# A planned attention and FFN kernel: slack between engines past the first units, and a lead of three

## The chip, the cores and the metric

The kernel runs on one core of a Trainium2 chip. The metric is the device time of one execution in microseconds. Five engines matter here: TensorE (PE) multiplies matrices, VectorE (DVE), ScalarE (ACT) and GpSimd (POOL) work on elements, and SyncE (SP) issues the DMA transfers. Each engine runs its own instructions in the order in which the program lists them, and waits on semaphores for what other engines make.

## The reference, cut to what matters

```python
def _attn_ref(q, k, v):                       # (4, 8, 768, 64)
    k_sum = k.reshape(B, H, nb, 32, D).max(axis=3)
    v_sum = v.reshape(B, H, nb, 32, D).mean(axis=3)
    scores_l = scale * q @ k.T                # kept where |i - j| < 16
    scores_s = scale * q @ k_sum.T + log(32)
    a = softmax(concat(scores_l masked, scores_s))
    return a @ concat(v, v_sum)

def _moe_ref(x, w_in, w_out):                 # x (3072, 512), d_ff 2048
    h = x @ w_in
    g = h * (1.0 / (1.0 + np.exp(-h)))
    return g @ w_out
```

The attention of 4 batches and 8 heads gives 3072 tokens of 512 numbers, and a feed-forward network (FFN) with a hidden width of 2048 follows.

## The kernel before, in words

Attention works in 24 stages s of 128 tokens, six to a batch. A stage has four score groups m (two heads each): PE makes the scores (L544 for batch 0, L546 and L547 for the others), DVE adds the mask and takes the maximum (L551), ACT takes the exponential (L554), DVE the reciprocal of the sum (L559, L560). The weights p are then written as float16 by DVE, ACT or POOL (one helper: L569 on DVE, L565 on ACT, L567 on POOL), and DVE makes their low parts (L593, four instructions a group). A transposing DMA (L596) turns p, PE multiplies with v (L625, 40 matmuls a stage), and ACT and DVE write the result as xh and xl (L643, L644; L638, L639 in the first two stages). The q, k and v of batches 1 to 3 come by DMA and are split into two parts by ACT, DVE and POOL (L444 to L450, L506, L507, L210, L215).

The FFN works in units: 12 chunks c of 256 tokens times 16 slices f of the hidden width, 192 units. The list `order` sets their sequence: chunk 0 and chunk 1 with the first eight slices, then with the other eight, then chunks 2 to 11 one after another. Unit i is done by `job_f`:

- F1 (L699): 12 matmuls of 256 columns into a PSUM bank of a ring of three (two for chunks 0 and 1);
- tanh on ACT (L709) into a tile t of a ring of three;
- t = (t + 1) * h on DVE (L710), the last reader of the bank;
- gh, the rounded part, on ACT (L711), and gl, the rest, on POOL or DVE (L215), each in a ring of four;
- F2 (L704): two halves of three matmuls of 512 columns, into two PSUM banks that collect the chunk; at its end ACT or DVE copies them out (L730, L731).

Nothing of this is issued where it stands in the code. Each step is entered with `plan.op`: which engines may do it and its cost on each, what it reads and writes, and a priority. `Plan.schedule` makes a list schedule from these costs, `sweep`, forward and backward in turns, and `issue` writes the instructions out by planned start. The time from the end of one operation to the start of the next that needs it is `lag`: on one engine `SELF`, else `LAT` and small additions. The planned times are used for the order and for the choice of the engine alone; on the chip the semaphores decide. PE also gets filler matmuls (L285, L708) where the plan sees a gap in the first part.

The tuning numbers (`TUNE`) and the costs of the operations are the same in both kernels. Line numbers of the text are those of the kernel before; in the changed kernel L699 is L704, L704 is L709, L710 is L715, and L569 is L574.

Of the kernel before, what the change touches and what calls it, by code (L numbers as in the profile page):

```python
# [44 lines left out]
LAST = (2.0 ** -29 * (1 - 2.0 ** -8), -0.5 + 7.5 * 2.0 ** -8)  # L45
QF = 8
AHEAD = 0
NPL = 2
NSUP = 2


class Plan:
# [19 lines left out]
    def __init__(self, tc, fill):  # L72
        self.tc, self.fill = tc, fill
        self.ops, self.writer, self.readers = [], {}, {}

    def op(self, engines, fn, r=(), w=(), prio=0.0, cols=0, port=("dve", "pool"), fill=None):
        i = len(self.ops)
        deps = set()
        for key in r:
            deps.add(self.writer[key])  # L80
            self.readers.setdefault(key, []).append(i)
        for key in w:
            if key in self.writer:
                deps.add(self.writer[key])
            deps.update(self.readers.pop(key, ()))
            self.writer[key] = i
        deps.discard(i)
        self.ops.append((engines, fn, sorted(deps), prio, cols, port, fill))

    def lag(self, a, b):  # L90
        return (self.SELF if a == b else self.LAT)[a] + (self.LEAD if b == "dma" else 110 if b == "pe" and a != "pe" else 0)

    def stream(self, seen, t, cost, cols):

# [14 lines left out]
    def sweep(self, prio, on, back):  # L109

        n = len(self.ops)
        before, after = [o[2] for o in self.ops], self.users
        if back:
            before, after = after, before
        left = [len(d) for d in before]
        end, chosen = [0.0] * n, [None] * n
        free = {} if back else {"dma": 1680.0}
        shared = 0.0
        ready, seen, fills, filled, early, order = {}, {}, 0, self.FIRST, True, []

        def arrive(i):
            ready[i] = {e: max([end[d] + (self.lag(e, chosen[d]) if back else self.lag(chosen[d], e)) for d in before[i]], default=0.0)
                        for e in ((on[i],) if on else self.ops[i][0])}

        for i in range(n):
# [76 lines left out]
def local_attn_ffn(ctx: ExitStack, tc: tile.TileContext, qkT, qF, qD, kF, kD, v, vR, w, out):  # L202
# [113 lines left out]
    def nudge(tag, *at):  # L316
        return NUDGE.get("_".join((tag,) + tuple(str(x) for x in at)), 0.0)
# [369 lines left out]
    def job_f(i, c, f):  # L687
# [13 lines left out]
        def ffn2(u):  # L701
            def go(e):
                for q, (g, part) in enumerate(((gh, 0), (gh, 1), (gl, 0))):
                    nc.tensor.matmul(out=bank[ob[u]], lhsT=g[:, u * P:u * P + P], rhs=wt[f, 1][:, part, :], start=(opens and q == 0), stop=(closes and q == 2))  # L704
            return go

        plan.op({"pe": 1430}, ffn1, r=[(x, z, half) for x in ("xh", "xl") for half in range(2)] + [("w", f, 0), ("wl", f, 0)], w=[("bank", k)], prio=i + nudge("f1", i), cols=3072,
                fill=lambda: nc.tensor.matmul(out=h, lhsT=unit[:, :P], rhs=unit, start=True, stop=True))  # L708
        plan.op({"act": 264}, lambda e: nc.scalar.activation(out=t, in_=h, func=AF.Tanh, scale=0.5), r=[("bank", k)], w=[("t", j)], prio=i - TUNE["post"])  # L709
        plan.op({"dve": 335}, lambda e: nc.vector.scalar_tensor_tensor(out=t, in0=t, scalar=1.0, in1=h, op0=ALU.add, op1=ALU.mult), r=[("bank", k)], w=[("t", j)], prio=i - TUNE["post"], port=())  # L710
        plan.op({"act": 307}, lambda e: nc.scalar.copy(out=gh, in_=t), r=[("t", j)], w=[("gh", n)], prio=i - TUNE["post"])  # L711
        plan.op({"pool": 742, "dve": 340}, lambda e: less(e, gl, t, gh.bitcast(F32)), r=[("t", j), ("gh", n)], w=[("gl", n)], prio=i - TUNE["post"])
        for u in range(2):
            plan.op({"pe": 690}, ffn2(u), r=[("gh", n), ("gl", n), ("w", f, 1), ("wl", f, 1)], w=[("bank", ob[u])], prio=late, cols=1536)
        if closes and f == NFT - 1:  # L715
            stg, key = staging()
        for u in range(2 if closes else 0):
# [61 lines left out]
    for f in range(NFT):  # L779
        for kind in range(2):  # L780
            job_w(f, kind, need_f[f] - TUNE["w_dec"] + kind)
    for i, (c, f) in enumerate(order):
        d = min([d for d in range(c + 1, NCHUNK) if slot[d] == slot[c]], default=None)
        if d and f == (QF if c < NSUP else AHEAD):
            job_stage(2 * d)
            job_attn(2 * d, True)
            job_stage(2 * d + 1)
        job_f(i, c, f)
        if c == 0 and f == NFT - 1:
            spare[0] = 1  # L790
        if d and f == NFT - 1:
            job_out(2 * d, True)
            job_attn(2 * d + 1, True)
            job_out(2 * d + 1, True)
# [73 lines left out]
```

## Time and profile before

| | |
|---|---|
| median of 3 runs | 691.08 us (690.7 to 693.31) |
| the profiled execution | 690.36 us |
| its span, first to last instruction | 688.6 us |
| PE busy | 662.1 us, 96% |
| DVE, ACT, POOL busy | 488.3, 427.3, 213.5 us |
| data moved by DMA | 97.43 MB, mean 141 GB/s |

The span is the stretch that the trace covers; the time of the execution is a little longer. Busy is the time in which at least one instruction of an engine runs. Matmuls are pipelined, so one takes longer from start to end than it holds up the next one; the busy time of PE is therefore read with the weight loads (PEld) and the waits beside it.

### The profile page before, as it was taken

How to read it: one execution, taken by the hardware profiler on the slowest of the kernel's cores; microseconds unless marked ns; L12 is line 12 of the kernel's file. 1: busy time of each engine (PE TensorE's matmuls, PEld its weight loads, DVE VectorE, ACT ScalarE, POOL GpSimd, SP SyncE). 2: the span in 40 equal slices, each digit the busy share in tenths (PEclk: the TensorE clock that was granted, in tenths of full speed). 3: DMA queues.
4: the chain of work that ended last, by engine and by line, in shares of the span. 5: the costliest groups of instructions: out<-in, count | busy, mean ns of one | idle time of the engine just before them, and what ended most of it. 6: DMA issues, size and time to landing. Idle time of an engine off the chain costs nothing. (4 is left out here: it accounts for less than half of the span.)

```text
span 688.6 us, 14268 instructions
## 1 busy us (share of the span) xinstructions
PE 662.1 (96%) x4971; PEld 572.1 (83%) x4971; DVE 488.3 (71%) x1500; ACT 427.3 (62%) x1136; POOL 213.5 (31%) x265
## 2 busy tenths in 40 slices
PE   8989999998999999999899999989999999999997
PEld 3668888887987988988788988977888888999996
DVE  5897978599988458887987556999996694323222
ACT  5988997686867547656756545676673584332222
POOL 3143465233645234234342242434333222000000
PEclk9999999999999999999999999999999999999999
DMA  8889863957666643754566532764573252000000
GB/s 275 257 243 302 320 221 104 251 161 215 132 152 149 210 116 97 171 135 111 157 158 156 179 102 79 182 160 113 123 187 75 73 126 61 12 31 1 30 1 32
DMA packets 101355, 97.43 MB, mean 141 GB/s; under 512 B 76950, under 2 KB 80022, under 8 KB 101282
## 3 DMA queue, kind: packets, MB, share of 16 engines
q1 hardware_dynamic: 101282, 96.51, 51.3%
q8 instruction: 39, 0.64, 0.4%
q14 instruction: 34, 0.28, 0.1%
HBM read 70.34 MB, written 6.29 MB: 111 GB/s over the span
## 5 line engine op out<-in xcount | busy, mean ns | idle before, releaser
L699 PE MATMUL bank<-xh,wt 128*128 128x256 f32 x1536 | 302.3, 287 | 8.1 <-DVE t L710 7.3
L699 PEld LDWEIGHTS bank<-xh,wt 128*128 128x128 f32 x1536 | 248.9, 192 | 18.0 <-DVE t L710 11.8
L704 PE MATMUL bank<-wt,gh 128*128 128x512 f32 x768 | 244.5, 400 | 1.9 <-DVE raw L731 1.9
L699 PE MATMUL bank<-xl,wt 128*128 128x256 f32 x768 | 218.3, 284 | 0.4 <-DVE xl L644 0.4
L215 POOL TENSOR_TENSOR gl<-t,gh 128x256 fp32r<-128x256 f32 x117 | 104.8, 900 | 254.6 <-ACT gh L711 206.0
L704 PEld LDWEIGHTS bank<-wt,gh 128*128 128x128 f32 x768 | 134.9, 189 | 24.3 <-DVE raw L731 2.1
L699 PEld LDWEIGHTS bank<-xl,wt 128*128 128x128 f32 x768 | 147.7, 192 | 3.8 <-DVE xl L644 0.8
L704 PE MATMUL bank<-wt,gl 128*128 128x512 f32 x384 | 150.0, 391 | 0.0
L711 ACT CAST gh<-t 128x256 fp32r<-128x256 f32 x192 | 75.8, 399 | 73.6 <-PE bank L704 67.5
L710 DVE SCALAR_TENSOR_TENSOR t<-t,bank 128x256 f32<-128x256 f32 x192 | 79.1, 417 | 54.9 <-ACT t L709 53.8
L709 ACT ACTIVATE t<-bank 128x256 f32<-128x256 f32 x192 | 71.3, 377 | 57.6 <-DVE gl L215 29.4
L593 DVE SCALAR_TENSOR_TENSOR p<-e,sum,p 128x128 f16<-128x128 f32 x352 | 104.8, 359 | 2.4 <-ACT p L565 1.7
L554 ACT ACTIVATE e<-e,mx 128x182 f32<-128x182 f32 x192 | 84.1, 439 | 24.5 <-DVE mx L551 24.2
L704 PEld LDWEIGHTS bank<-wt,gl 128*128 128x128 f32 x384 | 72.1, 188 | 16.2 <-POOL gl L215 0.2
L215 DVE TENSOR_TENSOR gl<-t,gh 128x256 fp32r<-128x256 f32 x75 | 45.1, 601 | 50.1 <-ACT gh L711 48.1
L567 POOL TENSOR_SCALAR p<-e,sum 128x182 f16<-128x182 f32 x68 | 33.8, 502 | 91.4 <-DVE sum L560 33.0
L551 DVE CUSTOM_DVE_ANT_0 e<-bank,masks,qsc 128x182 f32<-128x182 f32 x144 | 52.8, 400 | 8.3 <-PE bank L547 7.8
L565 ACT ACTIVATE p<-e,sum 128x182 f16<-128x182 f32 x79 | 32.6, 441 | 17.0 <-DVE sum L560 9.3
L215 POOL TENSOR_TENSOR vv<-raw,vv 128x1024 f16<-128x1024 f32 x16 | 34.6, 2168 | 14.7 <-DVE vv L212 11.1
L554 ACT ACTIVATION_READ_ACCUMULATOR e<-e,mx 128x1 f32 x192 | 36.1, 188 | 0.0
L450 DVE SCALAR_TENSOR_TENSOR qk<-raw,qsc,qk 64x1264 f16<-64x1264 f32 x18 | 28.1, 1561 | 6.5 <-ACT qk L449 6.0
L546 PE MATMUL bank<-qk 128*128 128x182 f16 x144 | 29.1, 247 | 2.6 <-DVE mx L551 2.0
(125 smaller groups left out, 687.4 us busy)
## 6 DMA issues: line engine op xcount, KB each, us to landing
wt<-in_w_dram SPq DMA_DIRECT2D x32, 512.0 KB
raw<-in_kD_dram SPq DMA_DIRECT2D x18, 632.0 KB
raw<-in_v_dram SPq DMA_DIRECT2D x20, 512.0 KB
raw<-in_qD_dram SPq DMA_DIRECT2D x18, 512.0 KB
out_dram<-raw SPq DMA_DIRECT2D x24, 256.0 KB
raw<-in_kF_dram SPq DMA_DIRECT2D x12, 384.0 KB
raw<-in_qF_dram SPq DMA_DIRECT2D x9, 512.0 KB
raw<-in_vR_dram SPq DMA_DIRECT2D x12, 384.0 KB
```

Source lines behind the costliest of these rows:

```text
L215: eng[e].tensor_tensor(out=out, in0=in0, in1=in1, op=ALU.subtract)
L546: nc.tensor.matmul(out=sc[:, i, :NKEY], lhsT=qh[:, h, :], rhs=kst[:, h, :], start=True, stop=False)
L551: plan.op({"dve": 258 if b == 0 else 323}, lambda e, i=i: nc.vector.tensor_tensor_reduce(out=et[:, i, :], in0=sc[:, i, :NKEY], in1=mask, s ...
L554: plan.op({"act": 431}, lambda e, i=i, h=h: nc.scalar.activation(out=et[:, i, :], in_=et[:, i, :], func=AF.Exp, scale=-1.0, bias=mx[:, i:i ...
L565: nc.scalar.activation(out=out, in_=et[:, i, :], func=AF.Copy, scale=by)
L567: nc.gpsimd.tensor_scalar(out=out, in0=et[:, i, :], scalar1=by, scalar2=0.0, op0=ALU.mult, op1=ALU.add)
L593: nc.vector.scalar_tensor_tensor(out=pt[:, i, to:to + z - a], in0=et[:, i, a:z], scalar=su[:, i:i + 1], in1=pt[:, i, a:z], op0=ALU.mult, o ...
L699: nc.tensor.matmul(out=h, lhsT=wt[f, 0][:, part, ct * P:(ct + 1) * P], rhs=x[:, ct, :], start=(ct == 0 and q == 0), stop=(ct == NCT - 1 an ...
L704: nc.tensor.matmul(out=bank[ob[u]], lhsT=g[:, u * P:u * P + P], rhs=wt[f, 1][:, part, :], start=(opens and q == 0), stop=(closes and q == 2))
L709: plan.op({"act": 264}, lambda e: nc.scalar.activation(out=t, in_=h, func=AF.Tanh, scale=0.5), r=[("bank", k)], w=[("t", j)], prio=i - TUN ...
L710: plan.op({"dve": 335}, lambda e: nc.vector.scalar_tensor_tensor(out=t, in0=t, scalar=1.0, in1=h, op0=ALU.add, op1=ALU.mult), r=[("bank", ...
L711: plan.op({"act": 307}, lambda e: nc.scalar.copy(out=gh, in_=t), r=[("t", j)], w=[("gh", n)], prio=i - TUNE["post"])
```

## The change

Three things are added, all in the plan. Operations that belong to attention or to the loading of data carry, from unit 32 on (`SETTLED`), a slack: where an operand comes from another engine, `lag` adds 2500 ns when the reader runs on PE, and 800 ns when it runs on DVE, ACT or POOL. No slack is added between operations of one engine, or for a reader on the DMA queue. The operations of `job_f` get 800 ns on PE alone (`GATE_SLACK`). And a key `turn` makes F1 of unit i depend on the second half of F2 of unit i - 3 (`APART`), in all units from 3 on. Both are on PE, so this costs no instruction and no semaphore.

```diff
--- before.py
+++ after.py
@@ -45,7 +45,11 @@
 LAST = (2.0 ** -29 * (1 - 2.0 ** -8), -0.5 + 7.5 * 2.0 ** -8)
 QF = 8
 AHEAD = 0
+SETTLED = 32
+SLACK = {"pe": 2500, "dve": 800, "act": 800, "pool": 800}
+GATE_SLACK = 800
 NPL = 2
+APART = 3
 NSUP = 2
 
 
@@ -72,6 +76,7 @@
     def __init__(self, tc, fill):
         self.tc, self.fill = tc, fill
         self.ops, self.writer, self.readers = [], {}, {}
+        self.slack = {}
 
     def op(self, engines, fn, r=(), w=(), prio=0.0, cols=0, port=("dve", "pool"), fill=None):
         i = len(self.ops)
@@ -85,10 +90,10 @@
             deps.update(self.readers.pop(key, ()))
             self.writer[key] = i
         deps.discard(i)
-        self.ops.append((engines, fn, sorted(deps), prio, cols, port, fill))
-
-    def lag(self, a, b):
-        return (self.SELF if a == b else self.LAT)[a] + (self.LEAD if b == "dma" else 110 if b == "pe" and a != "pe" else 0)
+        self.ops.append((engines, fn, sorted(deps), prio, cols, port, fill, dict(self.slack)))
+
+    def lag(self, a, b, user):
+        return (self.SELF if a == b else self.LAT)[a] + (self.LEAD if b == "dma" else 110 if b == "pe" and a != "pe" else 0) + (0 if a == b else self.ops[user][7].get(b, 0))
 
     def stream(self, seen, t, cost, cols):
 
@@ -119,7 +124,7 @@
         ready, seen, fills, filled, early, order = {}, {}, 0, self.FIRST, True, []
 
         def arrive(i):
-            ready[i] = {e: max([end[d] + (self.lag(e, chosen[d]) if back else self.lag(chosen[d], e)) for d in before[i]], default=0.0)
+            ready[i] = {e: max([end[d] + (self.lag(e, chosen[d], d) if back else self.lag(chosen[d], e, i)) for d in before[i]], default=0.0)
                         for e in ((on[i],) if on else self.ops[i][0])}
 
         for i in range(n):
@@ -704,14 +709,14 @@
                     nc.tensor.matmul(out=bank[ob[u]], lhsT=g[:, u * P:u * P + P], rhs=wt[f, 1][:, part, :], start=(opens and q == 0), stop=(closes and q == 2))
             return go
 
-        plan.op({"pe": 1430}, ffn1, r=[(x, z, half) for x in ("xh", "xl") for half in range(2)] + [("w", f, 0), ("wl", f, 0)], w=[("bank", k)], prio=i + nudge("f1", i), cols=3072,
+        plan.op({"pe": 1430}, ffn1, r=[(x, z, half) for x in ("xh", "xl") for half in range(2)] + [("w", f, 0), ("wl", f, 0)] + ([("turn", i - APART)] if i >= APART else []), w=[("bank", k)], prio=i + nudge("f1", i), cols=3072,
                 fill=lambda: nc.tensor.matmul(out=h, lhsT=unit[:, :P], rhs=unit, start=True, stop=True))
         plan.op({"act": 264}, lambda e: nc.scalar.activation(out=t, in_=h, func=AF.Tanh, scale=0.5), r=[("bank", k)], w=[("t", j)], prio=i - TUNE["post"])
         plan.op({"dve": 335}, lambda e: nc.vector.scalar_tensor_tensor(out=t, in0=t, scalar=1.0, in1=h, op0=ALU.add, op1=ALU.mult), r=[("bank", k)], w=[("t", j)], prio=i - TUNE["post"], port=())
         plan.op({"act": 307}, lambda e: nc.scalar.copy(out=gh, in_=t), r=[("t", j)], w=[("gh", n)], prio=i - TUNE["post"])
         plan.op({"pool": 742, "dve": 340}, lambda e: less(e, gl, t, gh.bitcast(F32)), r=[("t", j), ("gh", n)], w=[("gl", n)], prio=i - TUNE["post"])
         for u in range(2):
-            plan.op({"pe": 690}, ffn2(u), r=[("gh", n), ("gl", n), ("w", f, 1), ("wl", f, 1)], w=[("bank", ob[u])], prio=late, cols=1536)
+            plan.op({"pe": 690}, ffn2(u), r=[("gh", n), ("gl", n), ("w", f, 1), ("wl", f, 1)], w=[("bank", ob[u])] + ([("turn", i)] if u else []), prio=late, cols=1536)
         if closes and f == NFT - 1:
             stg, key = staging()
         for u in range(2 if closes else 0):
@@ -780,12 +785,15 @@
         for kind in range(2):
             job_w(f, kind, need_f[f] - TUNE["w_dec"] + kind)
     for i, (c, f) in enumerate(order):
+        plan.slack = SLACK if i >= SETTLED else {}
         d = min([d for d in range(c + 1, NCHUNK) if slot[d] == slot[c]], default=None)
         if d and f == (QF if c < NSUP else AHEAD):
             job_stage(2 * d)
             job_attn(2 * d, True)
             job_stage(2 * d + 1)
+        plan.slack = {"pe": GATE_SLACK} if i >= SETTLED else {}
         job_f(i, c, f)
+        plan.slack = SLACK if i >= SETTLED else {}
         if c == 0 and f == NFT - 1:
             spare[0] = 1
         if d and f == NFT - 1:
```

How it moves instructions is seen at three places. The first is PE in the last chunks, past all score groups: the first matmul of each F1 (L699 before, L704 in the changed kernel; its bank is the output) and the first of each F2 (L704 before, L709 in the changed kernel; gh3 is the tile of unit 171, gh0 that of unit 172). Units 172 to 175 before:

```order
L699 MATMUL bank2_201<-xh1_185,wt_1297 128x256
...
L699 MATMUL bank0_199<-xh1_185,wt_1341 128x256
...
L699 MATMUL bank1_200<-xh1_185,wt_1401 128x256
...
L704 MATMUL bank4_203<-wt_943,gh1_192 128x512 x2
...
L704 MATMUL bank4_203<-wt_966,gh2_193 128x512 x2
...
L704 MATMUL bank4_203<-wt_1048,gh3_194 128x512 x2
...
L699 MATMUL bank2_201<-xh1_185,wt_1468 128x256
```

and units 172 to 175 in the changed kernel:

```order
L704 MATMUL bank2_201<-xh1_185,wt_1220 128x256
...
L709 MATMUL bank4_203<-wt_1145,gh2_193 128x512 x2
...
L704 MATMUL bank0_199<-xh1_185,wt_1298 128x256
...
L709 MATMUL bank4_203<-wt_1183,gh3_194 128x512 x2
...
L704 MATMUL bank1_200<-xh1_185,wt_1331 128x256
...
L709 MATMUL bank4_203<-wt_1267,gh0_191 128x512 x2
...
L704 MATMUL bank2_201<-xh1_185,wt_1418 128x256
```

Before, three F1 stand together and then the six halves of three F2; the F2 that stand between F1 of 174 and of 175 are those of units 169, 170 and 171 (gh1, gh2, gh3), and that of 172 comes after F1 of unit 177. In the changed kernel F1 and F2 take turns, and between F1 of units 172 and 173 stands F2 of unit 170.

The second place is PE before the first F1: fillers (L285 and L708; L290 and L713 in the changed kernel), scores (L544; L549), products with v (L610; L615), and F1 of unit 0. Before:

```order
L285 MATMUL bank0_199<-ident_96 128x256
L544 MATMUL bank6_205<-qk0_149 128x182 x2
L708 LDWEIGHTS ident_96
L708 MATMUL bank0_199<-ident_96 128x256
...
L708 MATMUL bank0_199<-ident_96 128x256
L699 MATMUL bank0_199<-xh0_184,wt_446 128x256
```

and in the changed kernel:

```order
L290 MATMUL bank0_199<-ident_96 128x256
L549 MATMUL bank6_205<-qk1_150 128x182 x2
L615 MATMUL bank7_206<-wt_92,wt_91 64x128 x8
...
L549 MATMUL bank6_205<-qk1_150 128x182 x2
...
L549 MATMUL bank6_205<-qk1_150 128x182 x2
L713 LDWEIGHTS ident_96
L713 MATMUL bank0_199<-ident_96 128x256
...
L713 MATMUL bank0_199<-ident_96 128x256
L704 MATMUL bank0_199<-xh0_184,wt_386 128x256
```

Before, a score group on qk0, which is the first of stage 4, stands directly ahead of F1 of unit 0, with three fillers between; in the changed kernel that group comes after F1 of unit 1, and four fillers are left.

The third place is DVE in the attention of batch 2, around the group with e0 and sum0: the reciprocal (L560; L565 in the changed kernel), p (L569; L574), its low parts (L593; L598), t (L710; L715). Before:

```order
L710 SCALAR_TENSOR_TENSOR t0_188<-t0_188,bank1_200 128x256
L559 TENSOR_SCALAR sum2_168<-sum2_168 128x2
L593 SCALAR_TENSOR_TENSOR p_175<-e0_172,sum0_166,p_175 128x128
...
L593 SCALAR_TENSOR_TENSOR p_175<-e0_172,sum0_166,p_175 128x54
L710 SCALAR_TENSOR_TENSOR t1_189<-t1_189,bank2_201 128x256
L560 RECIPROCAL sum2_168<-sum2_168 128x2
L569 TENSOR_SCALAR p_175<-e2_174,sum2_168 128x182
L593 SCALAR_TENSOR_TENSOR p_175<-e2_174,sum2_168,p_175 128x128
```

and in the changed kernel:

```order
L565 RECIPROCAL sum0_166<-sum0_166 128x2
L565 RECIPROCAL sum1_167<-sum1_167 128x2
L574 TENSOR_SCALAR p_175<-e0_172,sum0_166 128x182 x2
L574 TENSOR_SCALAR p_175<-e1_173,sum1_167 128x182
L598 SCALAR_TENSOR_TENSOR p_175<-e0_172,sum0_166,p_175 128x128
...
L598 SCALAR_TENSOR_TENSOR p_175<-e0_172,sum0_166,p_175 128x54
L715 SCALAR_TENSOR_TENSOR t1_189<-t1_189,bank2_201 128x256
```

Before, p of this group is made by another engine and DVE makes p of the next one alone; in the changed kernel DVE makes both weights of this group itself, and one of the next. Over the whole program p stands on DVE 88 times in the changed kernel and 29 before, on ACT 46 and 79, on POOL 42 and 68 (times of L569, L565 and L567 into p); all other counts move by a few, and the fillers go from 103 and 4 to 73 and 8.

## Rows read from the trace of the kernel before

**Rows 1.** The page: span, and busy time of four engines (share, instructions).

```profile
span 688.6 us, 14268 instructions
...
PE 662.1 (96%) x4971; PEld 572.1 (83%) x4971; DVE 488.3 (71%) x1500; ACT 427.3 (62%) x1136; POOL 213.5 (31%) x265
```

**Rows 2.** The chain that ended last: start us, us, what.

```profile
539.37 0.08 PE bank L547
...
605.83 1.24 PE bank L625 x40
...
644.42 2.87 PE bank L699 x24
647.29 2.07 PE bank L704 x9
```

**Rows 3.** Waits of PE from 161.9 us: who, for whom, us, times, longest.

```profile
PE bank L699 <- DVE t L710: 6.2, 10, 1.6
...
PE bank L546 <- DVE mx L551: 1.6, 1, 1.6
```

**Rows 4.** Waits of the weight loads (PEld) from 161.9 us.

```profile
PEld bank L699 <- DVE t L710: 10.2, 13, 2.1
...
PEld bank L704 <- DVE raw L731: 2.1, 1, 2.1
PEld bank L412 <- DVE vm L404: 1.6, 1, 1.6
PEld bank L383 <- DVE am L379: 1.1, 2, 0.6
```

**Rows 5.** Waits of all engines over the whole span, the longest that concern the FFN.

```profile
ACT gh L711 <- PE bank L704: 67.5, 38, 4.5
...
ACT t L709 <- DVE gl L215: 29.4, 46, 2.2
```

**Rows 6.** Timeline, 242 to 250 us: start, us, instruction [idle before <-releaser].

```profile
243.08 2.12 DVE L215 TENSOR_TENSOR gl<-t,gh 128x256 fp32r<-128x256 f32 x1 [0.28 <-issue]
...
245.22 0.38 ACT L709 ACTIVATE t<-bank 128x256 f32<-128x256 f32 x1 [2.24 <-DVE gl L215]
...
247.53 0.39 ACT L709 ACTIVATE t<-bank 128x256 f32<-128x256 f32 x1 [1.62 <-DVE gl L215]
...
249.19 0.41 DVE L710 SCALAR_TENSOR_TENSOR t<-t,bank 128x256 f32<-128x256 f32 x1
...
249.66 0.38 PE L699 MATMUL bank<-xh,wt 128*128 128x256 f32 x1 [0.25 <-DVE t L710]
```

**Rows 7.** Timeline at the first F1: PE, and the xl that it reads.

```profile
48.59 0.68 DVE L639 TENSOR_TENSOR xl<-bank,xh 128x512 fp32r<-128x512 f32 x1
...
49.98 0.85 PE L544 MATMUL bank<-qk 64*128 64x182 f32 x4 [2.08 <-DMA qk<-in_qkT_dram]
...
51.24 0.56 PE L699 MATMUL bank<-xh,wt 128*128 128x256 f32 x1
```

**Rows 8.** Two windows: length, busy by engine, PEclk, DMA share, GB/s.

```profile
50.80:54.20 3.40, 3.40 (x18) 3.27 (x18) 3.22 (x10) 2.73 (x4) 0.79 (x1) 0.50 0.68 219
340.90:344.30 3.40, 3.40 (x19) 3.30 (x18) 3.37 (x10) 3.08 (x13) 1.84 (x3) 0.50 0.43 117
```

**Rows 9.** Groups by line: count | busy us, mean ns | idle before.

```profile
L593 DVE SCALAR_TENSOR_TENSOR p<-e,sum,p 128x128 f16<-128x128 f32 x352 | 104.8, 359 | 2.4 <-ACT p L565 1.7 <-POOL p L567 0.5
...
L711 ACT CAST gh<-t 128x256 fp32r<-128x256 f32 x192 | 75.8, 399 | 73.6 <-PE bank L704 67.5 <-DVE t L710 4.4
...
L569 DVE TENSOR_SCALAR p<-e,sum 128x182 f16<-128x182 f32 x29 | 11.8, 406 | 2.5 <-DMA tt<-p 1.6 <-DVE sum L560 0.3
```

**Rows 10.** One line's instructions: min/median/max ns, first to last start.

```profile
L593 DVE SCALAR_TENSOR_TENSOR p<-e,sum,p x352: 256/336/2253, 28.8 to 599.7; 128x128 f16<-128x128 f32 x176
...
L215 POOL TENSOR_TENSOR gl<-t,gh x117: 722/741/1965, 57.1 to 651.8; 128x256 fp32r<-128x256 f32 x117
...
L215 POOL TENSOR_TENSOR vv<-raw,vv x16: 2139/2148/2341, 90.2 to 516.4; 128x1024 f16<-128x1024 f32 x16
```

## The prediction

> **What bounds the kernel now.** I read the page first. PE is busy for 662.1 of 688.6 us, DVE for 488.3, ACT for 427.3, POOL for 213.5 [rows 1]. So PE sets the time, and an order can only win what PE loses in waits. The chain that ended last says the same from its end: from 605 us on it is PE alone, F1, F2 and a last product with v back to back, where 24 F1 matmuls take 2.87 us and nine F2 matmuls 2.07 us [rows 2]. A unit is thus 1.44 us of F1 and two halves of 0.69 us, 2.82 us in all; 40 products with v take 1.24 us, and one of the four score matmuls of a group 0.08 us.
>
> Then the waits, by PE's matmuls and by its weight loads. From 161.9 us, where unit 32 starts, the matmuls wait 6.2 us for "DVE t" ahead of F1, ten times, and the weight loads 10.2 us, thirteen times [rows 3, 4]. The two are the same waits seen twice: a matmul's end is modelled late, so the first is a lower bound, and the loads, which stand directly ahead of the matmul, give the better size. DVE's t is the last reader of the bank that the next F1 fills, so this is a wait for a free bank. Next come a copy of the output banks (2.1 us), the sum of v (1.6), the scale of v (1.1) [rows 4], and scores for the maximum (1.6) [rows 3].
>
> Why is t late, when a ring of three banks should give 7.0 us (three units less one F1)? The list of all waits shows it: ACT's cast to gh waits 67.5 us for F2, in 38 places, and ACT's tanh 29.4 us for gl on DVE [rows 5]. PE's order lets F1 run up to ten units ahead of F2 (the ring of four gh, three t and three banks all full), so gh waits until F2 four units back has freed a tile, and all that stands behind gh on ACT waits with it. The timeline shows one such run: a gl that takes 2.12 us instead of its usual 0.42 holds the tanh that needs its tile for 2.24 us, the next tanh waits 1.62, t starts at 249.19 and F1 at 249.66 [rows 6]. Where the F1 come in a burst, as they do (the order has up to seven in a row), the bank of the first must come free within 2.9 us.
>
> **The change part by part.** *The lead of three.* F1 of unit i now stands behind the second half of F2 of unit i - 3. When that F2 runs, its gl, gh and t are long done, so the bank and the t tile of unit i - 3 are free and gh of unit i - 4 too: F1 cannot wait for "DVE t" any more, and neither gh nor tanh for the rings. It costs no instruction. The gain is the bank wait, 6.2 us by the one row and 10.2 by the other [rows 3, 4]; I take 9, nearer the row of the loads.
>
> What it exposes: F2 now waits for its own gl. Before, 20 us of PE work stood between F1 and F2 of a unit. In the new order I count 5.6 us in the last chunks (F2, F1, F2, F1) and 4.5 to 7 elsewhere. The chain in that gap is tanh 0.38, t 0.41 [rows 6], gh 0.40 [rows 9] and gl 0.74 on POOL [rows 10]: 1.9 us, some 2.3 with the hand-overs. So a delay of 3.3 us on ACT, DVE and POOL together is covered by the two units between; what is later stops PE. What is in front of t on DVE then counts. I added, from the new order, every DVE instruction between two t by the mean of its group, less 0.06 us each, because neighbours overlap by that (L593: mean 359 ns, but 104.8 / 352 = 298) [rows 9]. Over the old order this gives 486 us, where the page has 488.3. In the new order it gives 499. Against PE's work in the same stretches: units 24 to 40 DVE 56.6, PE 51.9; 64 to 96 DVE 96.0, PE 104.1; 112 to 152 DVE 128.4, PE 131.0; the rest is well below. So the first of them is short of DVE by 4.7 us, of which the cover takes some 3, and the third runs at 98%, where single lumps (xl, the splits of q and k, a late DMA ahead of them on ACT) will stop PE at times. I put down 2 for the first, 1 for the second and 2 for the third: 5 us of new waits, with bounds of 0 and 25 (below).
>
> *The slack of 2500 ns on PE.* Scores, products and the small scale matmuls of attention now stand later behind what they read. In the waits of the loads that is 1.6 for the sum of v and 1.1 for the scale [rows 4], together 2.7. I take 2.5; the lower bound is 0, should the tight places only move. The 1.6 us for the maximum [rows 3] fall in a stage that is still planned without slack and whose groups stand just as close; I leave them.
>
> *The output copy.* 2.1 us [rows 4], and soon after it comes one of two stretches of 3.4 us in which PE is granted half its clock, 1.2 GHz instead of 2.4 [rows 8]; that costs 1.7 us of work. At each end of a chunk an F1 now stands between the last F2 and the first of the next, 1.44 us in which the copy can run. I take 3.5 of the 3.8 together (0 if the copy is late all the same).
>
> *The slack of 800 ns on DVE, ACT and POOL.* It is charged only where an operand changes engine. The reciprocal is on DVE, so p on DVE is charged nothing and on ACT or POOL 800 ns: that is why DVE makes 59 more of them. At 0.41 us each [rows 9] less the overlap this is 20 us on DVE, partly given back by other moves; it is in the 499 above. It is hidden as long as DVE has gaps, and is the larger part of the new-wait bound where it has none.
>
> On p the trace and a rule differ in what they say. L593 takes 336 ns at the median and up to 2253, and POOL's subtraction for v takes 2148 [rows 10]. The Trainium skill (SBUF — State Buffer, Who interferes with whom) says that a DVE instruction with two SBUF inputs and a GpSimd instruction that reads SBUF exclude each other for a whole instruction. By it, 26 p fewer on POOL would spare DVE some blocking, while two more subtractions for v on POOL add up to 2.1 us each. The two nearly cancel and leave the sum as it is.
>
> *The start.* Until F1 of unit 0 neither slack applies, but the lead changes the planned priorities. Before, a score group of stage 4 waits 2.08 us for its DMA directly ahead of F1, which starts at 51.24, though xl was done at 48.59 + 0.68 = 49.27 [rows 7]. Now that group stands behind F1 of unit 1, and DVE's work up to that xl is the same within 0.3 us. F1 should start near 49.3. A half-clock stretch begins at 50.8 [rows 8], after the wait; it may go or move. I take 2.5 us (0 to 1.9 + 1.7 = 3.6).
>
> **The sum.** -9 - 2.5 - 3.5 - 2.5 + 5 = -12.5. The span goes from 688.6 to 676.1 us, and with the 1.8 us that lay around it the execution to 677.9. The median of three runs was 0.7 above the profiled one; I say 678.
>
> **The rivals.** *All gains, no new waits:* 10.2 + 2.7 + 3.8 + 3.6 = 20 off, 671 by the median. For it speaks that DVE's sum uses means, which hold some very long instructions; by L593's median, 336 ns [rows 10], the dense stretches are looser.
>
> *The waits only move:* F1 no longer waits for a bank, and F2 waits as long for gl, since what makes t late is not the order but ACT and DVE in front of it (the timeline's gl of 2.12 us is such a case). It then stands within 0.5% of before, about what a measurement here can tell from no change: 688 to 694, say 690. The Trainium skill (Perfetto Trace Analysis, Identifying Performance Opportunities) reads a repeated gap on the engine that should be full as too few buffers; by that the ring of three banks is the limit, and an order that keeps the ring earns nothing. Against it: 67.5 us of ACT's waits are for F2 itself [rows 5], which the order alone decides. Halfway to this case, with half of the gain gone, it is 684 to 687.5.
>
> *DVE becomes the bound, slower:* if DVE's neighbours do not overlap where it is dense, its sum by full means is 68 us in units 24 to 40, 116 in 64 to 96 and 128 in 120 to 152, against PE's 52, 104 and 106: 16 + 12 + 22 = 50 us in place of 5. With a lead of three PE follows DVE at once, and the time is 678 + 45 = 723; with half of the 50, which is the bound of 25 above, 698. It decides from the point at which DVE is 95% busy over 40 us on end; now it is at 71% over the whole [rows 1], and L593 with a mean of 359 ns and 298 of busy time each speaks against it [rows 9].
>
> **How the numbers follow.** The forecast, 672 to 684, has 0.55. All gains (671 or so, below 672) 0.13, half gone (684 to 687.5, still faster) 0.09, the waits move 0.13, slower 0.10. Faster by over 0.5%: 0.55 + 0.13 + 0.09 = 0.77; within: 0.13; slower: 0.10. For the range I leave out about one in ten on each side: 668 to 690; the forecast's own is 672 to 684.
>
> **What would show it.** The wait of F1 for "DVE t" at or near zero past unit 3, and ACT's gh for F2 likewise; these follow from the order, and their failing would mean that I misread it. In their place a wait of F2's loads for gl (POOL or DVE L220), 5 us in all, most of it in units 24 to 40 and 112 to 152. DVE busy near 500 us. F1 of unit 0 near 49.3 us. No half-clock stretch in mid kernel. The forecast is wrong if the F2 wait for gl goes past 15 us, or if DVE is at 95% over a stretch of 40 us; and the step most likely to fail is the size of the new waits, since three lumps in a row on DVE or a late DMA on ACT are in no sum of mine.

## The result, and the profile after

The changed kernel takes 681.9 us (median of four runs), the kernel before 691.4 us in four runs on the same chip: a ratio of 0.985, with a 95% interval of 0.983 to 0.988. So 1.5% of the time went, 9.5 us. The profiled execution took 681.8 us, with a span of 679.9 against 688.6. Of the kernels further down, slack_only ran twice in a slower state (700.32 and 701.69 us, granted clock 0.96 instead of 0.99), and these two runs are left out of its median.

The page of the changed kernel, span and busy times:

```profile
span 679.9 us, 14188 instructions
PE 660.3 (97%) x4945; PEld 571.1 (84%) x4945; DVE 500.8 (74%) x1550; ACT 417.2 (61%) x1103; POOL 215.4 (32%) x248
```

Beside [rows 1] PE does the same work, less 26 fillers, in a shorter span, and DVE is busy 12.5 us longer. The lines of the code moved by five: F1 is now L704, F2 L709, tanh L714, t L715, gh L716, gl L220, the scores L549, L551 and L552.

Waits of the changed kernel's matmuls from 125 us on, and below them those of its weight loads (engine, line, releaser, then us in total, times, longest):

```profile
PE bank L551 <- DVE mx L556: 5.1, 5, 1.6
PE bank L713 <- DVE t L715: 1.7, 1, 1.7
PE bank L709 <- POOL gl L220: 1.2, 2, 1.0
PE bank L709 <- DVE gl L220: 0.6, 1, 0.6
PE bank L709 <- ACT gh L716: 0.5, 2, 0.3
```

```profile
PEld bank L709 <- POOL gl L220: 4.0, 8, 1.4
...
PEld bank L709 <- ACT gh L716: 1.5, 3, 0.7
PEld bank L709 <- DVE gl L220: 1.3, 2, 1.0
```

The waits of F1 for t, 6.2 and 10.2 us in [rows 3, 4], are gone, and so are the output copy, the sum of v and the scale of v. Only a filler (L713) still waits for t once. New are F2's waits for gl and gh, and the scores of L551 wait 5.1 us for the maximum, all in units 31 to 40 but for one short one.

The waits of all engines in the changed kernel:

```profile
DVE t L715 <- ACT t L714: 100.9, 89, 2.6
ACT t L714 <- PE bank L704: 96.0, 85, 2.1
ACT gh L716 <- DVE t L715: 94.4, 125, 3.2
```

ACT's gh, which waited 67.5 us for F2 [rows 5], waits for t now: the chain of a unit is followed at once, step by step, as an order with a short lead makes it.

The start, on PE's timeline (start us, us, instruction, idle before it and releaser), and two windows of the half clock (length, then busy us of PE, PEld, DVE, ACT and POOL, granted clock, DMA share, GB/s):

```profile
47.45 1.04 PE L713 MATMUL bank<-ident 128*128 128x256 bf16 x4
48.14 0.56 PE L704 MATMUL bank<-xh,wt 128*128 128x256 f32 x1
50.39 0.58 PE L704 MATMUL bank<-xl,wt 128*128 128x256 f32 x1 [1.69 <-DVE xl L644]
```

```profile
44.40:54.60 10.20, 8.45 (x38) 6.67 (x37) 8.94 (x26) 9.42 (x24) 7.21 (x6) 0.50 0.90 252
51.20:54.60 3.40, 3.40 (x17) 3.40 (x17) 2.14 (x8) 3.40 (x10) 1.92 (x1) 0.50 1.01 366
```

The first F1 starts at 48.14 instead of 51.24 [rows 7], but its second matmul waits 1.69 us for xl, and PE runs at half its clock (1.2 GHz) for 10.2 us there, where it was 3.4 [rows 8].

For the rest of this text one more number is worked out from the matmuls' starts of each kernel. If every matmul is given the median distance from its start to the next one's of its kind (0.12 us for one of F1, 0.23 for one of F2), the matmuls of every kernel here, fillers left out, add up to 627.5 us. The time at a point, less the work done up to there, is called **lost**: it went into waits, half clock and the start. Before, 28.2 us were lost up to F1 of unit 16, 34.9 up to unit 40, 57.2 at the end. After, 26.7, 37.3 and 48.6. So the changed kernel loses more up to unit 40 (+2.4) and half as much behind it: 11.3 instead of 22.3.

### The profile page after: what moved, and what is told of

It is laid out like the page before. It is cut to its first block, busy times and chain, and to the rows that moved or that the text cites. A ratio compares the mean times of both kernels' runs of the same rounds, so it can differ in the third digit from the quotient of the medians.

```text
span 679.9 us, 14188 instructions
## 1 busy us (share of the span) xinstructions
PE 660.3 (97%) x4945; PEld 571.1 (84%) x4945; DVE 500.8 (74%) x1550; ACT 417.2 (61%) x1103; POOL 215.4 (32%) x248
## 4 chain that ended last, share of the span: by engine, by line
PE 61%; DVE 24%; ACT 6%; DMA 5%; issue 4%; POOL 1%; SPq 1%; ACTq 0%; DVEq 0%; POOLq 0%
PE bank L704 27%; PE bank L709 26%; DVE p L598 8%; DVE e L556 3%; DVE p L574 2%; PE bank L630 2%; DVE t L715 2%; ACT e L559 2%; DVE qk L450 1%; DVE qk L455 1%; PE bank L549 1%; DMA raw<-in_kF_dram 1%; PE bank L483 1%; DMA raw<-in_qF_dram 1%; DMA raw<-in_vR_dram 1%
## 5 line engine op out<-in xcount | busy, mean ns | idle before, releaser
L704 PE MATMUL bank<-xh,wt 128*128 128x256 f32 x1536 | 309.4, 285 | 0.0
L704 PEld LDWEIGHTS bank<-xh,wt 128*128 128x128 f32 x1536 | 252.6, 192 | 8.1 <-issue 0.4
L709 PE MATMUL bank<-wt,gh 128*128 128x512 f32 x768 | 247.0, 403 | 0.6 <-ACT gh L716 0.5
L704 PE MATMUL bank<-xl,wt 128*128 128x256 f32 x768 | 218.0, 284 | 1.7 <-DVE xl L644 1.7
L220 POOL TENSOR_TENSOR gl<-t,gh 128x256 fp32r<-128x256 f32 x118 | 105.0, 891 | 309.7 <-ACT gh L716 266.4
L715 DVE SCALAR_TENSOR_TENSOR t<-t,bank 128x256 f32<-128x256 f32 x192 | 79.8, 415 | 101.6 <-ACT t L714 100.9
L704 PEld LDWEIGHTS bank<-xl,wt 128*128 128x128 f32 x768 | 147.2, 192 | 8.3 <-DVE xl L644 2.0
L709 PE MATMUL bank<-wt,gl 128*128 128x512 f32 x384 | 150.8, 393 | 1.9 <-POOL gl L220 1.2
L709 PEld LDWEIGHTS bank<-wt,gh 128*128 128x128 f32 x768 | 130.4, 190 | 18.8 <-ACT gh L716 1.5
L716 ACT CAST gh<-t 128x256 fp32r<-128x256 f32 x192 | 77.3, 404 | 96.3 <-DVE t L715 94.4
L714 ACT ACTIVATE t<-bank 128x256 f32<-128x256 f32 x192 | 72.2, 377 | 96.2 <-PE bank L704 96.0
L598 DVE SCALAR_TENSOR_TENSOR p<-e,sum,p 128x128 f16<-128x128 f32 x352 | 117.2, 393 | 1.4 <-ACT p L570 0.8
L709 PEld LDWEIGHTS bank<-wt,gl 128*128 128x128 f32 x384 | 72.1, 188 | 21.7 <-POOL gl L220 4.3
L220 DVE TENSOR_TENSOR gl<-t,gh 128x256 fp32r<-128x256 f32 x74 | 36.8, 497 | 33.2 <-ACT gh L716 15.9
L220 POOL TENSOR_TENSOR vv<-raw,vv 128x1024 f16<-128x1024 f32 x18 | 40.7, 2263 | 16.0 <-ACT vv L213 8.2
L574 DVE TENSOR_SCALAR p<-e,sum 128x182 f16<-128x182 f32 x88 | 34.4, 421 | 0.8
L572 POOL TENSOR_SCALAR p<-e,sum 128x182 f16<-128x182 f32 x42 | 22.8, 550 | 37.5 <-DVE sum L565 28.2
L551 PE MATMUL bank<-qk 128*128 128x182 f16 x144 | 28.7, 245 | 5.1 <-DVE mx L556 5.1
L630 PEld LDWEIGHTS <-vv 128*64 128x64 f16 x880 | 25.2, 110 | 4.9 <-issue 3.1
```

What stands on the lines that cost most here:

```text
L220: eng[e].tensor_tensor(out=out, in0=in0, in1=in1, op=ALU.subtract)
L551: nc.tensor.matmul(out=sc[:, i, :NKEY], lhsT=qh[:, h, :], rhs=kst[:, h, :], start=True, stop=False)
L574: nc.vector.tensor_scalar(out=out, in0=et[:, i, :], scalar1=by, scalar2=None, op0=ALU.mult)
L598: nc.vector.scalar_tensor_tensor(out=pt[:, i, to:to + z - a], in0=et[:, i, a:z], scalar=su[:, i:i + 1], in1=pt[:, i, a:z], op0=ALU.mult, o ...
L630: nc.tensor.matmul(out=av[j * D:(j + 1) * D, i * P:(i + 1) * P], lhsT=vt[:, vi, h * D:(h + 1) * D], rhs=tt[:, j * 3 + blk, :], start=(n == ...
L704: nc.tensor.matmul(out=h, lhsT=wt[f, 0][:, part, ct * P:(ct + 1) * P], rhs=x[:, ct, :], start=(ct == 0 and q == 0), stop=(ct == NCT - 1 an ...
```

## Experiments: each half of the change

The first four kernels each take the changed kernel and alter one or two lines of it. The reason on trial was the prediction's: the bound on the lead frees the banks, and is the larger half.

**lead_only**, the bound without any slack:

```diff
-SLACK = {"pe": 2500, "dve": 800, "act": 800, "pool": 800}
-GATE_SLACK = 800
+SLACK = {}
+GATE_SLACK = 0
```

> The lead of three alone, no slack anywhere. If the lead is what pays (my theory): F1's wait for t past unit 32 and ACT's wait of gh for F2 are both near zero, as in the changed kernel, while scores and the small scale matmuls wait as before; 684 us, between 682 and 687. If the slack is what pays (rival): F2 waits for gl take the place of the bank waits, 689 to 692.

Measured: 693.97 us, ratio 1.007 (1.004 to 1.010). My 682 to 687 us failed: the bank waits are gone, and the kernel is slower than before. It is above the rival's 689 to 692 us too.

**slack_only**, the slacks without the bound:

```diff
-APART = 3
+APART = 1000
```

> Both slacks, no bound on the lead. My theory: PE runs ahead as before, gh waits for F2 again (over 40 us on ACT) and F1's weight loads wait for t 5 us or more; 686 to 689 us. Rival (the slack pays): the 800 ns on PE are enough to keep F1 off a busy bank, bank waits under 2 us, 681 to 683.

Measured: 685.38 us, ratio 0.993 (0.991 to 0.996). Waits of all engines in this kernel, and then the weight loads' waits of F1 from 180 to 670 us:

```profile
ACT gh L716 <- PE bank L709: 89.5, 61, 4.4
```

```profile
PEld bank L704 <- DVE t L715: 2.3, 2, 1.4
```

The time is just under the 686 to 689 us of my theory, and gh waits for F2 as it said. But the wait that the theory turns on is not there, which decides against my reason. ACT's gh waits longer for F2 than before (89.5 us against 67.5), the F1 still run up to ten units ahead, and yet F1 waits for t only 2.3 us from unit 40 on.

**lead_late** (the bound only from unit 32 on, the slacks as in the changed kernel) and **settled16** (the slacks from unit 16 on, the bound as in the changed kernel) asked whether the two halves are held back by where they begin:

```diff
-([("turn", i - APART)] if i >= APART else [])
+([("turn", i - APART)] if i >= SETTLED else [])
```

```diff
-SETTLED = 32
+SETTLED = 16
```

> The changed kernel with the lead of three from unit 32 on only, so that the first 32 units are planned nearly as before. If the lead is what costs time early (units 24 to 32 took 40.0 us in the changed kernel, 34.0 before, and the start ran 10 us at half clock): F1 of unit 40 is reached some 5 us earlier for the same work, 677 to 679 us. If the early loss is only work that has to be done somewhere (rival): what is saved there comes back as waits in units 32 to 64, 681 to 682.

> The changed kernel with slack from unit 16 instead of 32. If the 5 us of score waits for the maximum between 160 and 173 us are due to tight planning without slack: they fall below 2 us, 677 to 679 us. If DVE is short of time there (33.9 us of DVE work in units 24 to 32 against 29.6 of PE, rival): the waits move to F2 or to xl and the time stays 681 to 683.

Measured: 688.90 us, ratio 0.999 (0.997 to 1.002), and 691.23 us, 1.002 (1.000 to 1.005). Both expectations failed. Lost up to unit 40 and behind it, in us, show why: before 34.9 and 22.3; changed kernel 37.3 and 11.3; lead_only 41.1 and 19.6; slack_only 40.3 and 12.1; lead_late 41.9 and 13.7; settled16 44.3 and 11.6. Two things are mixed here. Behind unit 40, every kernel with the slack loses 11 to 14 us, and the one without loses 20. But the plan is made as one, so each edit also makes the start and the first 40 units anew, and all four came out 3 to 7 us worse there than the changed kernel.

## Experiments: the first 40 units held

So the other eight kernels hold the first 40 units. The planner first makes the plan of before. All operations that it places ahead of F1 of unit 40 are then issued in that order, and only the rest is planned with the slacks or the bound:

```diff
+KEEP = 40
     def schedule(self):
+        self.free = True
+        base = self.plan({}, ())
+        first = [o for o in sorted(base, key=lambda o: o[0]) if self.ops[o[2]][6]][KEEP]
+        head = [(o[2], o[3]) for o in sorted(base, key=lambda o: o[0]) if o[0] < first[0]]
+        self.kept = kept = {i for i, _ in head}
+        self.free = False
+        return self.plan({i: d for i, d in self.soft.items() if i not in kept}, head)
```

An operation in `kept` has no slack and no bound; `free` switches both off for the first plan. On PE all eight then issue the same as before up to F1 of unit 40 at least, and lose 34.8 to 36.7 us up to there. They differ from one another in these lines:

```
 graft_none      SLACK = {}    GATE_SLACK = 0     APART = 1000
 graft_lead      SLACK = {}    GATE_SLACK = 0     APART = 3
 graft_gate      SLACK = {}    GATE_SLACK = 800   APART = 1000
 graft_attn      SLACK = {"pe": 2500, "dve": 800, "act": 800, "pool": 800}    GATE_SLACK = 0     APART = 1000
 graft_attn_pe   SLACK = {"pe": 2500}                                         GATE_SLACK = 0     APART = 1000
 graft_attn_eng  SLACK = {"dve": 800, "act": 800, "pool": 800}                GATE_SLACK = 0     APART = 1000
 graft_slack     SLACK = {"pe": 2500, "dve": 800, "act": 800, "pool": 800}    GATE_SLACK = 800   APART = 1000
 graft_both      SLACK = {"pe": 2500, "dve": 800, "act": 800, "pool": 800}    GATE_SLACK = 800   APART = 3
```

First which half pays, and which slack:

**graft_slack.** 

> The plan of the kernel before is kept, operation by operation, up to the first products of unit 40; from there all slacks of the change hold, and no bound on the lead. So the start and the first 40 units cost what they cost before. Theory now (the slack, not the bound on the lead, took away the waits behind unit 40): PE's losses past unit 40 fall from 22.3 to about 12 us as in slack_only, so about 679.5 us (677 to 682), bank waits of first products under 3 us. Rival 1 (the prediction's: only the bound keeps the banks free): bank waits stay at 6 us or more, and only the scale and product waits of some 3 us go, 685 to 688 us. Rival 2 (what slack_only gained past unit 40 came from the other order it had reached by then): 688 to 691 us.

**graft_lead.** 

> The plan of before up to the first products of unit 40; from there the bound of three units alone, no slack. Theory now: the bank waits (8.3 us) go to zero, but score, scale and half waits take most of their place as in lead_only, where the losses past unit 40 were 19.6 us against 22.3: 687 us (685 to 690). Rival 1 (the prediction's lead term, -9 us, held for these units and was covered up in lead_only by the worse first 40 units): 680 to 683 us.

**graft_gate.** 

> The plan of before up to the first products of unit 40; from there only the 800 ns that first products and second products keep to results of other engines, no slack for the attention's own operations, no bound on the lead. Theory now: this is the slack that frees the banks, since the first products that write a bank keep 800 ns behind DVE's t, so the bank waits fall from 8.3 to under 2 us while scale and product waits stay: 682.5 us (680 to 685). Rival 2: the 800 ns are too few beside waits of 0.6 to 0.7 us each and DVE's delays, bank waits stay over 4 us: 686 to 690 us.

**graft_attn.** 

> The plan of before up to the first products of unit 40; from there only the slack of the attention's operations (2500 ns on PE, 800 on the others), nothing on the first and second products, no bound on the lead. Theory now: the waits for scale, masked rows and halves (some 5 us past unit 40) go, the bank waits of 8.3 us stay: 685.5 us (683 to 688). Rival 2 (the attention's results come late on PE and push all that follows, the bank waits among them, so that this slack is the whole gain): 679 to 682 us.

Then a control, the whole change, and the attention's slack in two parts:

**graft_none.** 

> A control. The plan of before up to the first products of unit 40, and from there a plan made anew with no slack and no bound on the lead: what the making anew does by itself. Theory now (the attention's slack pays): 690 us (687 to 692), losses past unit 40 of 19 to 23 us, with bank waits of 6 us or more. Rival (any new plan behind unit 40 would have gained, because the old one was unlucky there): under 684 us.

**graft_both.** 

> The plan of before up to the first products of unit 40; from there the slacks and the bound of three units, so the whole change for these units and nothing of it ahead of them. Theory now: with the slack there, the bound gives nothing and costs its waits of second products for gl, 3 to 5 us more than graft_slack: 679.5 us (677 to 682). Rival (the prediction's: the bound still removes the 2.2 us of bank waits that graft_slack keeps, and gl comes in time): 673 to 676 us.

**graft_attn_pe.** 

> The plan of before up to the first products of unit 40; from there only PE's 2500 ns for the attention's operations, without the 800 ns of the other three engines. Theory now: DVE, ACT and POOL seldom wait for one another on the path, so PE's 2500 ns carry the gain of graft_attn (12.5 us) nearly whole: 680.5 us (678 to 683). Rival (it is the 800 ns that let DVE's queue run free of waits, so that t is in time for the banks): 686 to 690 us.

**graft_attn_eng.** 

> The plan of before up to the first products of unit 40; from there only the 800 ns that the attention's operations on DVE, ACT and POOL keep, nothing on PE. Theory now: PE goes on waiting for scales, maxima and masked rows, and DVE's t for the banks stays late: 687.5 us (685 to 690). Rival (the 800 ns free DVE's queue): 679 to 682 us, bank waits under 4 us.

Measured: median and ratio to before on the same chip (95%); "lost" is that behind unit 40. "PE idle" is 490 us less PE's busy time in the window from 180 to 670 us. "DVE held" is the sum of DVE's waits in that window without those of its t and gl, that is, the time in which DVE's queue stood still behind an operation of attention, of a load or of an output copy. The last three columns come from one profiled execution of each kernel. Before, it took 690.36 us, 2 to 3 us less than the medians here; for graft_none it took 2.9 us more than the median and for graft_attn_eng 2.1 more, so small differences in these columns tell nothing. graft_gate, graft_lead, graft_attn and graft_slack ran beside the 692.46 us, the other four, on another chip, beside the 693.54.

| kernel | us | ratio | lost | PE idle | DVE held |
|---|---|---|---|---|---|
| before | 692.46 and 693.54 | 1 | 22.3 | 10.8 | 63.8 |
| graft_none | 694.81 | 1.001 (0.999 to 1.003) | 28.2 | 15.3 | 78.9 |
| graft_gate | 691.73 | 0.999 (0.997 to 1.002) | 21.7 | 10.6 | 60.5 |
| graft_lead | 688.96 | 0.995 (0.993 to 0.996) | 20.5 | 10.9 | 49.3 |
| graft_attn_pe | 687.75 | 0.995 (0.992 to 0.998) | 17.3 | 7.9 | 45.5 |
| graft_attn_eng | 681.85 | 0.983 (0.980 to 0.987) | 13.9 | 5.8 | 14.0 |
| graft_attn | 679.93 | 0.981 (0.978 to 0.984) | 11.4 | 5.6 | 21.8 |
| graft_both | 677.20 | 0.976 (0.973 to 0.980) | 8.1 | 1.7 | 6.9 |
| graft_slack | 675.59 | 0.975 (0.972 to 0.978) | 7.0 | 1.7 | 23.9 |

What follows. The new planning by itself gives nothing (graft_none; its 694.81 us are above the range that I gave, 687 to 692). The bound alone gives 0.5%. The slack alone gives 2.5%, and the bound on top of it nothing that can be measured, since the intervals of graft_slack and graft_both, taken on two chips, overlap. So the theory that the slack pays held, with a larger gain than I expected. But which slack pays was a miss twice. I expected it of the 800 ns on the first and second products, which stand between DVE's t and F1: graft_gate gives nothing by itself. On top of the attention's slack it does give something: graft_slack, which is graft_attn with the 800 ns of graft_gate, is 4.3 us faster on the same chip, and none of its six runs is as slow as the fastest of graft_attn. And I expected it of PE's 2500 ns: they give 0.5%, and the 800 ns of DVE, ACT and POOL give 1.7%. The rivals of graft_attn, graft_attn_pe and graft_attn_eng were right; that of graft_gate was right on the bank waits (9.5 us by the loads, over its 4), but 691.73 us is slower than its 686 to 690.

The rows behind it. Waits of DVE from 180 to 670 us, those of the attention, in the kernel before:

```profile
DVE xl L644 <- ACT xh L643: 9.2, 7, 4.9
DVE e L551 <- PE bank L547: 7.8, 7, 3.0
DVE vv L215 <- ACT vv L208: 7.2, 2, 7.0
DVE qk L450 <- ACT qk L449: 6.0, 5, 2.4
DVE sum L559 <- ACT e L554: 5.0, 6, 1.9
DVE qm L339 <- ACT raw L338: 4.1, 2, 3.5
DVE vv L212 <- ACT raw L506: 3.7, 1, 3.7
```

and in graft_attn_eng, where its own 800 ns and those of ACT and POOL stand ahead of the same operations:

```profile
DVE e L575 <- PE bank L571: 3.3, 4, 1.5
DVE xl L668 <- ACT xh L667: 3.2, 3, 2.9
DVE km L351 <- DMA raw<-in_kF_dram: 3.1, 2, 1.7
DVE qc L373 <- PE bank L369: 1.6, 1, 1.6
```

Before, vv, qk, sum and qm cost DVE 26 us in these rows; in graft_attn_eng none of them is among the larger waits. The weight loads of F1 wait for t 3.6 us there instead of 10.2 (first row; L723 is F1), and in graft_slack 2.6 (second row):

```profile
PEld bank L723 <- DVE t L734: 3.6, 5, 1.3
```

```profile
PEld bank L723 <- DVE t L734: 2.6, 3, 1.1
```

One of the places in the kernel before, on DVE's, ACT's and PE's timeline, where F1 of unit 144 is due:

```profile
525.08 0.42 DVE L710 SCALAR_TENSOR_TENSOR t<-t,bank 128x256 f32<-128x256 f32 x1 [0.45 <-ACT t L709]
529.18 0.69 DVE L212 CAST vv<-raw 128x1024 f16<-128x1024 f32 x1 [3.68 <-ACT raw L506]
529.91 1.64 DVE L215 TENSOR_TENSOR vv<-raw,vv 128x1024 f16<-128x1024 f32 x1
531.48 0.41 DVE L710 SCALAR_TENSOR_TENSOR t<-t,bank 128x256 f32<-128x256 f32 x1
```

```profile
528.00 1.15 ACT L506 ACTIVATE raw<-raw,vsc 128x1024 f32<-128x1024 f32 x1 [2.95 <-DMA raw<-vms]
...
530.50 0.38 ACT L709 ACTIVATE t<-bank 128x256 f32<-128x256 f32 x1 [0.75 <-POOL gl L215]
```

```profile
531.94 0.39 PE L699 MATMUL bank<-xh,wt 128*128 128x256 f32 x1 [1.02 <-DVE t L710]
```

ACT stands 2.95 us at a scaling of v whose DMA has not landed. DVE stands 3.68 us at the split that reads it, and then takes 2.3 us for the split. The t behind it ends at 531.9 and PE, which needs its bank, has been idle for a microsecond. My reading is that the plan had put L506 and L212 just where their operands were due, and that a slack of 800 ns puts other work ahead of them; the trace does not hold the planned times, so this is not shown. What it shows is that the operands came late, and that what stood behind them on both engines was late with them.

Not told apart: which of the three engines' 800 ns does it, and by which way. The path over DVE's queue is read from these rows, and one kernel fits it badly: in graft_attn_pe DVE is held for 45.5 us instead of 63.8, and F1's loads still wait 10.8 us for t. The slack also moves work from engine to engine. DVE writes 75 whole p in graft_attn_eng, 93 in graft_attn, 89 in graft_both and 95 in graft_slack, but 24 to 31 before and in the held kernels without the 800 ns. No run keeps the choice of engines and changes the order alone, so the margin and the shift of p from ACT and POOL to DVE are not separated. ACT's own waits outside the chain of a unit go from 95.6 to 55.2 us in graft_attn_eng too, those on DMAs among them from 37.1 to 12.9. Nor did a run show which part of the plan is too short, a duration or a landing.

graft_slack is the best kernel of this study, 2.5% faster than before, where the whole change, in runs on another chip, was 1.5% faster. By the lost time the difference between the two is 1.9 us up to unit 40 and 4.3 behind it.

## Why the prediction was right, and where not

Forecast were 678 us in a range of 668 to 690; it is 681.9. By stretches of the program, from the lost time: the start up to unit 16 was to give 2.5 and gave 1.5; units 16 to 40 were to cost 2 (the first of the new waits) and cost 3.9; behind unit 40 the other terms add up to -12, and -11.0 were measured. Together -12.5 and -8.6.

*The lead of three, -9.* The waits went as forecast, but what paid was mostly not the bound. F1's waits for t did go, 10.2 us by the loads. But the bound by itself, with the start held, gives 3.8 us (0.55% of 692.46; graft_lead), since second products (L728), the scale of v (L407, which waits for am) and scores (L570) wait there, as these rows of its weight loads and of its matmuls from 180 to 670 us show:

```profile
PEld bank L728 <- POOL gl L239: 3.7, 5, 1.3
...
PEld bank L407 <- DVE am L403: 2.7, 2, 1.6
```

```profile
PE bank L570 <- DVE mx L575: 2.4, 4, 1.2
```

PE is idle for 10.9 us in the window, as before. And the slack takes 7.6 of the 10.2 us without any bound (graft_slack). The step that failed is the explanation: "all that stands behind gh on ACT waits with it". That wait is real, but it does not by itself make t late. It grows to 87.0 us in graft_slack, the fastest kernel, as this row of its waits shows:

```profile
ACT gh L735 <- PE bank L728: 87.0, 62, 4.4
```

A gh that waits for F2 does so when PE is far ahead with its F1, and has F2 left to do. So the total came near in part by luck: most of what I had booked for the bound was earned by the slack, which I had booked as a cost. With the start held the bound alone is worth 3.8 us and the slack alone 16.9.

That F1 cannot wait for t any more past unit 3 was wrong for one place: a filler matmul (L713) waits 1.7 us at 131.3 us, in the first 32 units, where the ring has two banks and not three. I had argued with three.

*The slack of 800 ns.* Here lies the gain, and I put it down as a cost alone: more p on DVE. The cost is there too. DVE makes 88 whole p instead of 29 [rows 9], and its busy time is 500.8 where I had 499 to 500. But in graft_slack DVE makes 95 of them and is busy for 487.7 us, as long as before, and PE is idle for 1.7 us. So the cost did not show there, and the shift of p to DVE may even be part of the gain. Nor did the rule of the Trainium skill (SBUF — State Buffer, Who interferes with whom) show in the time; no run isolates that rule. L593's mean of 359 ns is 393 in the changed kernel, with 18 subtractions for v on POOL, and 354 in graft_slack with 14; but before had 16 and 359.

*PE's slack, -2.5, the output copy and half clock, -3.5.* None of these waits is left, and no half clock stands in mid kernel, as predicted. That PE's slack and the bound removed them is not shown: the waits for the sum of v and for the scale of [rows 4] are gone in graft_attn_eng too, where PE has no slack, and the wait for the output copy is gone in graft_none, where nothing was added (with three stretches of half clock at other waits).

*The start, -2.5.* F1 came even earlier than forecast (48.1 for 49.3), but it had been put ahead of its xl: 1.69 us of wait inside F1, and the half clock three times as long. The gain up to unit 16 was 1.5.

*New waits, +5.* 6.8 us by the loads past 125 us: next to none in units 24 to 40, 2.0 in units 48 to 52, 1.0 at 83, 3.8 in 135 to 153. The third place came, larger than put down (2); the first did not: there, where DVE was to be short, the scores waited for the maximum instead (5.1 us, where I had left 1.6 as it was). These 3.5 us in place of the 2 put down make 1.5 of the 1.9 us by which units 16 to 40 missed; the start and the units behind 40 missed by 1.0 each. The rival in which DVE becomes the bound did not come, though the sign that I had set for it did, DVE at 95% over 40 us. Two windows of 40 us, the first in the changed kernel, the second in graft_slack (length, busy us of PE, PEld, DVE, ACT and POOL, granted clock, DMA share, GB/s):

```profile
500.50:540.50 40.00, 38.63 (x321) 33.13 (x319) 39.64 (x121) 25.07 (x73) 18.18 (x18) 1.00 0.60 137
```

```profile
340.00:380.00 40.00, 40.00 (x341) 35.73 (x336) 38.81 (x117) 24.28 (x73) 16.80 (x17) 1.00 0.58 140
```

DVE is busy for 99% and 97% of them, and PE idle for 1.4 us in the one and never in the other, so the sign was badly chosen. The rival in which the waits only move did happen, but with the bound alone: PE is as idle in graft_lead as before, and lead_only is no faster. With the slack they did not just move: PE is idle for 1.7 us in graft_slack and in graft_both.

The rule that I set beside that rival, that gaps which repeat on the engine that should be full can mean too few buffers (the Trainium skill, Perfetto Trace Analysis, Identifying Performance Opportunities), is not borne out here: in graft_slack the ring is the same, F1 runs as far ahead, and the waits for its banks fall from 10.2 to 2.6 us.

## What to carry to other kernels

When an engine waits for another's result, look at what stood ahead of that result in the other engine's queue and what that waited for: a queue in order passes each wait on, and the place to mend can be a third operation that waits for an operand itself. In a static plan try a margin between an operation and results of other engines, on the helping engines first: here it gave 1.7% on DVE, ACT and POOL (with p moved to DVE by it) and 0.5% on PE, the engine that sets the time. And when one rule is tested in a planner, hold the rest of the plan: here the new plan of the first 40 units moved the time by 2 to 9 us and hid a gain of 17.

## What the runs showed of the hardware

Half clock in mid kernel went with long waits of PE. In the 14 kernels profiled, between 180 and 670 us, the granted clock fell to 0.50 ten times, nine times for 3.41 us and once for 6.83. Each time the matmuls had just been idle, or were idle, for 1.6 to 5.2 us: 1.9 us for the output copy before, 3.0 for a maximum in graft_attn_eng, 5.2 for t in graft_none (the one of 6.83 us). Seven other idle times of 1.8 to 3.4 us were not followed by it. At half clock 3.41 us do 1.7 us of work, so a wait of 2 us that is followed by it costs nearly twice its length. The changed kernel, graft_slack and graft_both have no idle time of the matmuls over 1.5 us in that window and no half clock.

The same instructions in the same order do not start alike. The eight held kernels and the kernel before issue the same up to unit 40, and their first F1 starts between 51.2 and 53.9 us, with a half clock around it of 3.41 us in seven of the nine and 6.83 in two (graft_attn_pe, graft_attn_eng).
